# Splitting the inverse transform's turns and moving a weight load ahead in a mixer kernel

## The chip, the cores and the metric

The kernel runs on one core of a Trainium2 chip. The metric is device time in microseconds (us) of one execution, the median over several runs. The core has a matrix engine (TensorE, PE in the profile, its weight loads PEld), a vector engine (VectorE, DVE), an activation engine (ScalarE, ACT), a general engine (GpSimd, POOL), and a queue engine (SyncE, SP) that here issues nearly all DMAs. Every engine works through its own instructions in the order in which they were written. Results of TensorE go to PSUM, a small memory from which ACT and DVE copy them out ("evacuate" them) to SBUF.

## The reference

All inputs are fp32: a sequence of 2048 positions with 640 channels. Two blocks follow each other, each with a normalisation whose scale, shift and output factor come from a small product (`mod`, six rows of 640).

```
mod = silu(c) @ w_mod                  # sa, ca, ga, sb, cb, gb
h = layernorm(x) * (1 + ca) + sa
kv = shortconv(k, 4 taps) * v
y  = longconv(kv, ssm_k) + kv * ssm_D  # causal, 2048 taps, per channel, by FFT
x  = x + ga * (h * y)
h = layernorm(x) * (1 + cb) + sb
u = gelu(w1^T @ layernorm(h) + b1)     # along the positions: 2048 -> 1728
x = x + gb * (w2^T @ u + b2)           # 1728 -> 2048
```

## The kernel before

**Step one** makes the long convolution in 5 chunks of 128 channels (`for c in range(NC)`, c = 0 to 4; the last one has `cn is None`). Each chunk is a transform factored into 64 by 32 points. `step1` (products at L230) makes the first factor for the data (side 0) and for the filter (side 1), four turns each, and ACT copies each turn to the tile `z` (L235). `f2` (L249) makes the second factor in eight turns g = 0 to 7; ACT copies the filter's half (`kt`, L253), DVE multiplies (`mul`, tile `p`), and POOL or DVE adds up the complex product into the tile `y`. `i2` (products L279, copies L287) and `i1` (products L298) go back. `i2` is called twice per chunk, for r = 0 and 1: 128 products into two PSUM tiles of 128x1024 (`pp`), then four copies of 128x512 to `T2`, which lies in the tile `z`. The products of one `i2` go through s = 0 to 7, and s lies in blocks of 64 columns in each 512-column half of a tile. `i1` is called for both halves of the positions, 128 products into one PSUM tile each. Then `gate` (DVE) multiplies that tile with the normalised input `A1` (tile `aux`), and `add_x` adds the product to x. `a1_ops` makes `A1`: 16 ACT operations (L305), and on DVE the scale and shift (`po`, with the tile `g`). `fill` is a list of DVE operations that `dv(n)` takes n of at places written into the loop: the short convolution of a later chunk, and, from chunk 3 on, the statistics of the second normalisation (`x1s`, L524).

PSUM tiles come from a ring of three slots (`ring`); a fourth slot, `tap`, holds the sums of `mod_part` (L362), the product for `mod`. `i2` takes two slots, every other step one. Between the two calls of `i2` in chunks 1 to 3 stands one turn of `step1`. ACT also has, in these chunks, the copy `perm` (L176) of the next filter, which is written after the second turn of `step1` and before `i2(0)`.

**The last chunk** also loads the weights of step two. The first four blocks of 128 columns of `w1` are loaded as four row sets, r = 0 to 3, of 1 MB each (`load_rows` L416, set 0 in parts L544), and every set is split for each block f into a rounded part on ACT (L422) and a rest on DVE (`split_rows`, tiles `wb`). Set 0 goes to the tile `x`, set 1 to `aux`, set 2 to `z`, set 3 to `p` when that tile is no longer used.

**Step two** begins with the second block's normalisation: 16 row tiles j, each made by a chain of small operations (`stats`, `root_in`, `root`, `norm1`, `times`, `mean`, `plus`, `square`, `half`, `rest`; L716 to L764). Their order is written out by hand as a list of short names with arguments. `products` (Q, L445) multiplies two row tiles at a time with the four blocks of weights. Before the first Q stands a row of products whose result is not used (L804, 24 of them). After that come the other blocks of `w1`, the GELU, and the second product by seven multiplications in place of eight (L1086).

The order in all queues is that of the program (`manual_schedule`). Waits are put in by the framework, from what each instruction reads and writes.

## Time and profile before

| | |
|---|---|
| median of 3 runs | 682.18 us (678.96 to 683.72) |
| the profiled execution's own time | 679.36 us |
| its span, first to last instruction | 677.6 us |
| mean granted TensorE clock | 0.99 |
| PE busy | 629.8 us, 93% |
| DVE busy | 513.0 us, 76% |
| ACT busy | 316.0 us, 47% |
| POOL busy | 143.4 us, 21% |

All stamps are microseconds from the start of the span. A line of the chain of waits gives the start, the length, and the engine, tile and line that held the end of the program; "issue" is time in which the engine waited for nothing that the profile shows. A line of the timeline gives start, length, engine, line, operation, output and inputs with their shapes, the count, and in brackets the idle time of that engine before it and what ended this. A line of the windows gives, for a stretch of time, the busy time of PE, PEld, DVE, ACT and POOL (each with its count), the granted TensorE clock (1.00 is full), the share of the DMA engines and the GB/s that they moved.

Step one's chunks lie at about 23 to 100 (0), to 146 (1), to 196 (2), to 246 (3) and to 296 us (4); step two's Q runs from 306.05 us, and its second product from 506.61 us.

### The profile page before, as it was taken

The numbers are of one execution on the slowest core, as the hardware profiler recorded it, in microseconds if no ns is written. First come the engines' busy times: TensorE is split into PE (matmuls) and PEld (weight loads), VectorE is DVE, ScalarE is ACT, GpSimd is POOL, SyncE is SP. The second block draws the span as 40 slices with busy tenths as digits, with TensorE's granted clock in tenths as the row PEclk, the third lists the DMA queues.
The fourth block names the chain that finished last, engine by engine and source line by source line (L and its number), as shares of the span: only waits on it lengthen the run. The fifth ranks groups of instructions, "written<-read, shape, count | busy, mean of one in ns | idle before, by whom it ended". The sixth has DMA issues, their size and how long they took to land.

```text
span 677.6 us, 20710 instructions
## 1 busy us (share of the span) xinstructions
PE 629.8 (93%) x9057; PEld 611.8 (90%) x9057; DVE 513.0 (76%) x862; ACT 316.0 (47%) x483; POOL 143.4 (21%) x116
## 2 busy tenths in 40 slices
PE   0699888999999999889999999999999999999997
PEld 0699678999989989668999999999999999999997
DVE  7677689979978757879993312854679888888886
ACT  0574674745645546557875223433334333333331
POOL 5298039526327228200000000000000000000000
PEclk9999989999999999979999999999999999999999
DMA  9977987655432522634005540686499554355601
GB/s 188 217 219 237 369 147 152 156 95 136 85 69 86 165 63 69 180 86 102 2 1 108 116 88 1 166 221 172 143 345 304 176 178 121 114 160 167 182 34 40
DMA packets 173552, 95.91 MB, mean 142 GB/s; under 512 B 89715, under 2 KB 163222, under 8 KB 173462
## 3 DMA queue, kind: packets, MB, share of 16 engines
q1 hardware_dynamic: 168914, 93.28, 52.9%
q10 hardware_dynamic: 4548, 1.31, 1.1%
q8 instruction: 71, 1.16, 0.7%
q14 instruction: 19, 0.16, 0.1%
HBM read 77.53 MB, written 17.04 MB: 140 GB/s over the span
## 4 chain that ended last, share of the span: by engine, by line
PE 69%; DVE 17%; POOL 3%; issue 3%; DMA 3%; SPq 3%; ACT 2%; ACTq 0%; DVEq 0%; POOLq 0%
PE pst L1086 25%; PE pst L445 17%; PE pst L230 9%; PE pst L249 6%; PE pst L279 5%; PE pst L951 3%; DVE tap L60 3%; PE pst L298 2%; POOL y L60 2%; DVE p L60 2%; DVE kt L60 2%; SPq L166 1%; DVE x L60 1%; DMA in<-in_A_k_dram 1%; POOL t L60 1%
## 5 line engine op out<-in xcount | busy, mean ns | idle before, releaser
L249 PEld LDWEIGHTS pst<-z,w 128*64 128x64 f32 x2560 | 94.8, 141 | 5.8 <-ACT z L235 3.3
L249 PE MATMUL pst<-z,w 128*64 128x64 f32 x2560 | 96.1, 240 | 4.1 <-ACT z L235 2.1
L60 POOL TENSOR_TENSOR y<-p 128x256 f32<-128x256 f32 x68 | 89.4, 1366 | 25.6 <-DVE p L60 25.3
L230 PE MATMUL pst<-v,x 128*64 128x128 f32 x640 | 46.0, 303 | 25.4 <-DVE x L60 23.3
L230 PEld LDWEIGHTS pst<-v,x 128*64 128x64 f32 x640 | 43.9, 220 | 26.2 <-POOL t L470 23.2
L235 ACT ACTIVATE z<-pst 128x1024 f32<-128x1024 f32 (+2 forms) x45 | 46.5, 1046 | 41.8 <-PE pst L230 24.1
L60 DVE TENSOR_TENSOR p<-pst,kt 128x512 f32<-128x512 f32 x80 | 52.0, 692 | 15.2 <-ACT kt L253 8.7
L253 ACT ACTIVATE kt<-pst 128x512 f32<-128x512 f32 x40 | 25.3, 633 | 44.7 <-PE pst L249 25.3
L279 PEld LDWEIGHTS pst<-v,y 32*128 32x128 f32 x1280 | 38.7, 190 | 5.8 <-issue 3.9
L279 PE MATMUL pst<-v,y 32*128 32x64 f32 x1280 | 40.4, 275 | 3.2 <-issue 2.3
L230 PE MATMUL pst<-v,p 128*64 128x128 f32 x640 | 36.7, 274 | 2.4 <-ACT p L176 1.8
L230 PEld LDWEIGHTS pst<-v,p 128*64 128x64 f32 x640 | 35.0, 137 | 2.9 <-ACT p L176 1.9
L1086 PE MATMUL pst<-r_z,m_w 128*128 128x320 f32 x198 | 37.2, 309 | 0.0
L60 DVE TENSOR_TENSOR tap<-tap,kt 128x512 f32<-128x512 f32 x51 | 35.6, 697 | 1.3
L60 DVE TENSOR_TENSOR kt<-in,tap 128x512 f32<-128x512 f32 x51 | 35.1, 688 | 1.5
L1086 PEld LDWEIGHTS pst<-r_z,m_w 128*128 128x128 f32 x198 | 31.1, 188 | 0.1
L287 ACT ACTIVATE z<-pst 128x512 f32<-128x512 f32 x38 | 21.4, 664 | 19.6 <-PE pst L279 19.5
L1023 ACT ACTIVATE m_w<-m_v 128x896 fp32r<-128x896 f32 x19 | 17.9, 948 | 23.2 <-DVE m_v L60 13.1
L298 PEld LDWEIGHTS pst<-z,v 64*64 64x64 f32 x1280 | 23.0, 148 | 5.3 <-issue 2.5
L298 PE MATMUL pst<-z,v 64*64 64x64 f32 x1280 | 24.8, 233 | 1.9 <-issue 1.1
L855 ACT ACTIVATE pst<-pst,sm 128x640 f32<-128x640 f32 x14 | 10.7, 766 | 32.5 <-PE pst L445 32.5
L60 DVE TENSOR_TENSOR m_w<-m_v,m_w 128x896 fp32r<-128x896 f32 x19 | 20.6, 1087 | 6.5 <-ACT m_w L1023 6.5
(302 smaller groups left out, 1435.5 us busy)
## 6 DMA issues: line engine op xcount, KB each, us to landing
x<-in_B_w_dram SPq DMA_DIRECT2D x18, 512.0 KB
m_v<-in_B_w_dram SPq DMA_DIRECT2D x20, 384.0 KB
aux<-in_A_ssm_k_dram SPq DMA_DIRECT2D x10, 512.0 KB
out_dram<-m_w SPq DMA_DIRECT2D x32, 160.0 KB
in<-in_A_k_dram SPq DMA_DIRECT2D x36, 128.0 KB
in<-in_A_v_dram SPq DMA_DIRECT2D x36, 128.0 KB
ts<-m_p SPq DMA_DIRECT2D x10, 320.0 KB
m_w<-xs SPq DMA_DIRECT2D x20, 160.0 KB
```

Source lines behind the costliest of these rows:

```text
L60: TT = lambda eng, o, a, b, op: eng.tensor_tensor(o, a, b, op=op)
L230: pe.matmul(ps[64 * ri:64 * ri + 64, o:o + 128], lhs, F1[:, 128 * ri:128 * ri + 128], start=True, stop=True)
L235: act.activation(Z[:, side, t, :, k0:k1].rearrange("p a k e -> p e a k"), ps.rearrange("p (e a k) -> p e a k", a=8, e=2)[:, :, :, k0:k1], ...
L249: pe.matmul(ps[64 * h:64 * h + 64, o:o + 64], W2[k1 // 32][:, 2 * (k1 % 32) + ri], rhs, start=True, stop=True)
L253: act.activation(kt.rearrange("p (m i) -> p m i", i=32), pv[:, :, 1], AF.Copy)
L279: pe.matmul(pp[qd // 2][:, o:o + 64], Y[p, ri, i:i + 2].rearrange("p i k -> p (i k)"), V2[p, 64 * ri:64 * ri + 64], start=ri == 0, stop=ri ...
L287: act.activation(o, i, AF.Copy)
L298: pe.matmul(ps[64 * b:64 * b + 64, 512 * e + 64 * jj:512 * e + 64 * jj + 64], V1[p, ri, n2], T2[p, :, 32 * ri + n2], start=ri == 0, stop=r ...
L445: pe.matmul(ps[0:m, h, 0:320], w_.bitcast(F32R), r_[:, 320 * h:320 * h + 320].bitcast(F32R), start=first and i == 0, stop=last and i == 2)
L951: pe.matmul(ps[n][:, h, 0:320], sets[n][:, j].bitcast(F32R), r[:, 320 * h:320 * h + 320].bitcast(F32R), start=j == 0 and r is hh, stop=j = ...
L1023: act.activation(W[n][0].bitcast(F32R), A[p, w_], AF.Copy)
L1086: pe.matmul(bank[n], w[:, i].bitcast(F32R), r.bitcast(F32R), start=m == 0 and k == 0, stop=m == 6 and k == 2)
```

## The change

Five edits, all in step one and the entry of step two:

- `i2` in all chunks: the products go first through the even s (e = 0), then through the odd ones (e = 1), and after each half stand two copies of 128x512, one from each PSUM tile. Before, four copies stood at the end.
- Row sets 2 and 3 are copied in DRAM during chunk 3 to a new array `wc`, ordered so that one row of it holds all that a partition gets; set 2 in eight DMAs of 128 KB, set 3 in two of 512 KB. Set 2 is then loaded at turn 4 of the last chunk into the half of `w0` that later holds block 0's rests, and split in place (`split_third`); set 3 into `p` after the loop. The load of set 3 at the entry of step two goes. The `mod` load that was in `p` goes to `z`.
- In the last chunk's loop, ACT's `a1_ops` come three per turn, and `po` is taken from the loop's turns 4 to 7 (DVE) and no longer stands after the loop. 25 of the statistics move from the loop's first turns to the end of chunk 3.
- `i1(0)` of the last chunk comes in three parts (2, 3 and 3 of its 8 steps), with `mod_part` 3 and 4, `mod_sum` and `mod_row` placed between them. The gate and the add for the last three rows of this half, and the store of the half (`spill`), move into step two's list ("gr"); the add goes from DVE to POOL.
- In step two's list, the splits for block 2 ("v") and for row set 3 ("wh", "wl") stand at other places, three of the four "wh" on ACT are done earlier, and the unused products before Q are 40 in place of 24.

```
     def i2(r, eng=None):
         pp = [psum(), psum()]
...
+        for e in range(2):
+            for a in range(4):
+                for ri in range(2):
+                    for qd in range(4):
+                        p, s = slice(32 * qd, 32 * qd + 32), 2 * a + e
+                        o, i = 512 * (qd % 2) + 64 * s, 2 * (8 * r + s)
+                        pe.matmul(pp[qd // 2][:, o:o + 64], Y[p, ri, i:i + 2].rearrange("p i k -> p (i k)"),
+                                  V2[p, 64 * ri:64 * ri + 64], start=ri == 0, stop=ri == 1)
+            for n in range(2):
+                o = T2.rearrange("p (q a) m e -> p e q a m", a=8)[:, e, 2 * n:2 * n + 2, 4 * r:4 * r + 4]
+                i = pp[n].rearrange("p (q a e m) -> p e q a m", q=2, a=4, e=2)[:, e]
+                if eng is not None and n:
+                    eng.tensor_scalar(o, i, 1.0, None, op0=ALU.mult)
+                else:
+                    act.activation(o, i, AF.Copy)
...
+    THIRD = {0: 2, 1: 0, 2: 3, 3: 1}
+
+    def copy_rows(r, b, f=0, n=4):
+        o, step_ = (2048, 512) if r == 3 else (512 * THIRD[f], 128)
+        sync.dma_start(dram(wc, 64 * b * 4096 + o, [[4096, 64], [step_, 4], [1, 128 * n]]),
+                       dram(w1, (16 * b + 4 * r) * F + 128 * f, [[32 * F, 64], [F, 4], [1, 128 * n]]))
+
+    def split_third(f, hi=True, lo=True):
+        n = THIRD[f]
+        t, (h_, l_) = blk[0][1][:, 4 * n:4 * n + 4], (t_[:, 8:12] for t_ in blk[f])
+        if hi:
+            act.activation(h_.bitcast(F32R), t, AF.Copy)
+        if lo:
+            TT(dve, l_.bitcast(F32R), t, h_, ALU.subtract)
...
+            if cn == NC - 1:
+                copy_rows(2, g % 2, g // 2, 1)
+                if g in (3, 6):
+                    copy_rows(3, g // 6)
...
-                dv(4 if g else len(fill) - 16)
-                if g == 5:
+                dv(len(fill))
+                if g == 4:
                     t = mem("w0", 4096, "wb0")
                     blk[0] = j16(t[:, 0:2048]), j16(t[:, 2048:4096])
-                if g in (5, 7):
-                    split_rows(1, T_aux[:, 0:2048], (0,), g == 5, g == 7)
+                    sync.dma_start(t[:, 2048:4096], wc[:, 0:2048])
+                if g >= 4:
+                    po.pop(0)()
+                if g == 6:
+                    split_rows(1, T_aux[:, 0:2048], (0,), True, False)
+                if g == 7:
+                    split_third(0)
+                    split_rows(0, X, (0,), True, False)
...
-            load_rows(2, T_z[:, 1920:3968])
-            mod_load(3, 4, P[:, 0:1920])
+            mod_load(3, 4, T_z[:, 1920:3840])
+            sync.dma_start(P, wc[:, 2048:4096])
...
-            split_rows(0, X, (0, 1, 3))
-            split_rows(1, T_aux[:, 0:2048], (1, 3))
-            run(po)
+            for f in (1, 3):
+                split_third(f)
+                split_rows(0, X, (f,))
+                split_rows(1, T_aux[:, 0:2048], (f,))
+            split_rows(0, X, (0,), False, True)
+            split_rows(1, T_aux[:, 0:2048], (0,), False, True)
         if c:
...
             i2(0)
             if cn is None:
-                split_rows(2, T_z[:, 1920:3968], (0, 1, 3), True, False)
-                split_rows(2, T_z[:, 1920:3968], (0, 1), False, True)
+                split_rows(3, P, (1, 3))
+                split_rows(3, P, (0,), True, False)
+                i2(1, dve)
                 mod_part(tap, 3, pl[3])
-                i2(1, dve)
...
-            dv(3)
+            dv(3 if cn < NC - 1 else 28)
...
-    mod_part(tap, 4, pl[4])
-    ps0 = i1(0)
+    ps0 = i1(0, jjs=range(2))
     s0, s1, s2 = ((uid[0] + i) % 3 for i in range(3))
-    mod_sum(tap, T_t[:, 0:640])
     gate(NC - 1, ps0, 0, dve, 0, 2)
     run(lambda j=j: stats(j) for j in (0, 1))
+    split_rows(0, X, (2,), True, False)
+    split_rows(1, T_aux[:, 0:2048], (2,), True, False)
+    split_third(2, True, False)
+    mod_part(tap, 4, pl[4])
+    i1(0, ps=ps0, jjs=range(2, 5))
+    mod_sum(tap, T_t[:, 0:640])
     root_in(0)
-    gate(NC - 1, ps0, 0, None, 2, 8)
+    gate(NC - 1, ps0, 0, None, 2, 5)
     root(0)
-    add_x(NC - 1, 0, dve, 2, 8)
-    spill(NC - 1, (0,))
-    load_rows(3, P)
+    add_x(NC - 1, 0, dve, 2, 5)
...
+    i1(0, ps=ps0, jjs=range(5, 8))
     ps = i1(1, s1)
...
-    for i in range(24):
+    for i in range(40):
...
+    def rest_of_half():
+        gate(NC - 1, ps0, 0, None, 5, 8)
+        add_x(NC - 1, 0, pool, 5, 8)
+        spill(NC - 1, (0,))
...
-            t 0 1 m 0 w2 0 p 0 1 s 0 1 st 2 3 q 1 gb 0 R 1 n 2 3 h 0 1
+            t 0 1 m 0 v 0 p 0 1 s 0 1 st 2 3 q 1 gr 0 gb 0 R 1 n 2 3 h 0 1
...
```

More of the change, by code (lines that the diff above doesn't have):

```diff
@@ L68, in mixer_kernel @@
     ts = drp.tile([5 * 128, 2560], F32, name="ts")
+    wc = drp.tile([128, 4096], F32, name="wc")
     ring = [0, 1, 2]
@@ L273, in i2, with i1 @@
         pp = [psum(), psum()]
[L274 to L292 removed]
+        for e in range(2):
[13 more added lines that the diff above has]
+                    act.activation(o, i, AF.Copy)
+    def i1(half, slot=None, ps=None, jjs=range(8)):
+        if ps is None:
+            ps = psum(slot)
+        for jj in jjs:
             for ri in range(2):
@@ L537, in mixer_kernel @@
             if c:
-                for f_ in ac[2 * g:2 * g + 2]:
-                    f_()
+                n_ = 2 if cn is not None else 3
+                for f_ in ac[n_ * g:n_ * g + n_]:
+                    f_()
+            if cn == NC - 1:
+                copy_rows(2, g % 2, g // 2, 1)
+                if g in (3, 6):
+                    copy_rows(3, g // 6)
             if cn is None and g < 4:
```

37 lines of the change are left out of this document (10 added, 27 removed).

## The prediction

> **What bounds the kernel now.** I read the page first, then the chain of waits in order of time, and then the timelines of single engines where the change touches them.
>
> ```profile
> span 677.6 us, 20710 instructions
> PE 629.8 (93%) x9057; PEld 611.8 (90%) x9057; DVE 513.0 (76%) x862; ACT 316.0 (47%) x483; POOL 143.4 (21%) x116
> ```
>
> The kernel itself took 679.36 us, its span 677.6 us. PE is busy for 93% of the span, so a change must free time in which PE waits, or in which it can't yet begin with what only PE limits. The chain of waits (start, length, engine, tile, line, count) shows both kinds. First chunk 3, which is as chunks 1 and 2, and then the end of the last chunk:
>
> ```profile
> 224.24 2.28 PE pst L230 x32
> 226.52 3.73 PE pst L279 x128
> 230.25 2.24 PE pst L230 x32
> 232.49 3.93 PE pst L279 x128
> 236.42 2.23 PE pst L230 x32
> 238.65 2.02 PE pst L298 x118
> 240.67 0.89 issue
> ...
> 275.04 3.58 PE pst L279 x120
> 278.62 1.21 PE tap L362 x12
> 279.83 2.06 PE pst L279 x63
> 281.88 2.26 issue
> 284.14 2.90 PE pst L279 x63
> 287.04 2.29 PE tap L362 x12
> 289.32 3.25 PE pst L298 x128
> ...
> 292.59 0.44 DVE aux L60
> ```
>
> In chunk 3 the chain is PE alone: a turn of `step1` (L230), `i2(0)` (L279), a turn, `i2(1)`, a turn, `i1` (L298), without a gap up to a stop of 0.89 us that the profile gives to no engine. Whatever PE loses here, the kernel loses. At the end of the last chunk PE also holds the chain, up to the first gate on DVE at 292.59 us. From there small DVE and ACT steps lead to the first product of step two. In the next fence the first two lines are from PE's timeline, the last from the windows (span, then busy time of PE, with its count).
>
> ```profile
> 298.77 5.28 PE L804 MATMUL pst<-wb,wb 128*128 128x320 f32 x24 [1.68 <-ACT kt L387]
> 306.05 7.33 PE L445 MATMUL pst<-r_z,wb 128*128 128x320 f32 x48 [1.99 <-ACT r_z L761]
> ...
> 352.00:420.00 68.00, 68.00 (x465) 67.99 (x464) 20.70 (x34) 23.71 (x37) 0.00 (x0) 1.00 0.41 78
> ```
>
> Step two's products begin at 306.05 us; from 352 to 420 us PE is busy for 68.00 of 68.00 us. So the gain that the change can make is the time by which the first product comes earlier, as long as DVE follows.
>
> **Part 1, the waits inside `i2`.** The change adds two copies between the two halves of each `i2`. They read the tiles into which the second half then writes, other columns of the same 512-column halves. The trace of before has no place where PE writes columns of a PSUM tile while another engine reads other columns of it. So the cost has two ends. If PE need not wait, it is nothing; it is not less, since behind both calls in chunks 1 to 3 PE goes on with a turn of `step1` at once and a shorter tail of copies releases nothing. If PE waits, it costs the two copies and whatever is queued ahead of them on ACT. The nearest rows for a PE write to a tile that ACT is emptying are these, ACT and then PE:
>
> ```profile
> 68.25 1.08 ACT L235 ACTIVATE z<-pst 128x1024 f32<-128x1024 f32 x1 [0.70 <-PE pst L230]
> ```
> ```profile
> 69.37 3.79 PE L279 MATMUL pst<-v,y 32*128 32x64 f32 x124 [0.62 <-ACT z L235]
> ```
>
> The copy ends at 69.33 us and PE goes on at 69.37 us. PE waits for the whole reading operation, and starts 0.04 us behind it. I take this end, the full wait. The Trainium skill ("PSUM — Partial Sum Buffer", section "PSUM bank collisions raise a hardware error") speaks against the change: engines must be kept apart by bank and quadrant, not by address, because an access to other columns of the same bank collides all the same. By that rule the wait stands in all ten calls and the sum is the one below, +8.4 us. By the rows alone it may also be nothing, -5.8 us in all, and that is the first rival.
>
> ACT in chunk 3:
>
> ```profile
> 227.55 2.09 ACT L176 ACTIVATE p<-aux 128x2048 f32<-128x2048 f32 x1
> 230.28 2.30 ACT L287 ACTIVATE z<-pst 128x512 f32<-128x512 f32 x4 [0.64 <-PE pst L279]
> ...
> 236.28 2.26 ACT L287 ACTIVATE z<-pst 128x512 f32<-128x512 f32 x4 [2.65 <-PE pst L279]
> ```
>
> The first half of `i2(0)` is half of 3.73 us: it ends at 226.52 + 1.87 = 228.39 us. ACT is then in `perm` until 227.55 + 2.09 = 229.64 us, which stands ahead of the copies. Two of the four copies take half of 2.30, 1.15 us, to 230.79 us; the second half of the products ends at 232.66 us, against 230.25 us before: +2.41 us. For `i2(1)` ACT is free (it waited 2.65 us for PE), so two copies of 2.26 / 2 = 1.13 us are added. One chunk loses 3.54 us. `perm` is of one size in all chunks:
>
> ```profile
> L176 ACT ACTIVATE p<-aux 128x2048 f32<-128x2048 f32 x5 | 10.5, 2096 | 1.8 <-POOL aux L60 1.8
> ```
>
> Chunks 1 to 3 have the same order, so they lose 3 x 3.54 = 10.6 us. Everything behind (gate, short convolution, the next chunk's `f2`) starts from `i1`, so it moves along.
>
> In chunk 0, PE and then ACT:
>
> ```profile
> 78.28 3.80 PE L279 MATMUL pst<-v,y 32*128 32x64 f32 x128
> ```
> ```profile
> 80.36 1.65 ACT L305 ACTIVATE aux<-xa,sm 128x128 f32<-128x128 f32 x4 [1.60 <-DVE sm L351]
> 82.11 2.17 ACT L287 ACTIVATE z<-pst 128x512 f32<-128x512 f32 x4
> ```
>
> The first half of `i2(1)` ends at 78.28 + 1.90 = 80.18 us; ACT is in four operations of `a1_ops` until 82.01 us, the two copies (half of 2.17) end at 83.10 us, the second half at 85.0 us instead of 82.08 us: 2.9 us for `mod_part` 4 and what hangs on it, `A1` and the gate. The short convolution behind these waits a little for data anyway:
>
> ```profile
> 99.91 0.70 DVE L60 TENSOR_TENSOR tap<-in,tap 128x512 f32<-128x512 f32 x1 [0.78 <-DMA in<-in_A_k_dram]
> ```
>
> That takes 0.78 us off, and the DVE work between leaves some slack. `i2(0)` of this chunk loses about 1.1 us ahead of products of `mod` that wait for their own loads. Bounds 0 and 2.9 us; I take 1.3 us, a little under the middle, because of these two covers.
>
> **Part 2, the last chunk up to the gate.** DVE gets `po` in turns 4 to 7, that is four operations for which it took 4.87 us after the loop. In the next fence are DVE's rows and then POOL's.
>
> ```profile
> 269.44 1.33 DVE L60 TENSOR_TENSOR p<-pst,kt 128x512 f32<-128x512 f32 x2 [1.01 <-POOL y L60]
> ...
> 271.76 1.29 DVE L60 TENSOR_TENSOR p<-pst,kt 128x512 f32<-128x512 f32 x2 [0.40 <-ACT kt L253]
> 272.97 2.52 DVE L60 TENSOR_TENSOR y<-p 128x128 f32<-128x128 f32 x4
> ...
> 278.42 4.87 DVE L60 TENSOR_TENSOR aux<-aux,g 128x1024 f32<-128x1024 f32 x4
> ```
> ```profile
> 256.06 18.59 POOL L60 TENSOR_TENSOR y<-p 128x256 f32<-128x256 f32 x14 [6.17 <-DVE p L60]
> ```
>
> A turn of `f2` lasts about 2.4 us (14 additions of POOL, seven turns, in 18.59 us make 2.66 us), the multiplication takes 1.3 us of DVE and one `po` 1.22 us: DVE is just full, but POOL sets the pace, and DVE waited 1.01 us for it at 269.44 us. At turn 7 DVE then has the multiplication (to 270.7), `po` (to 272.0) and a split that waits for ACT (to 272.9 or so) before the last multiplication, which began at 271.76 us. About 1.2 us late, its first two additions (two of the four in 2.52 us) end near 275.5 us; POOL ends at 274.65 us. So `i2(0)` starts at 275.6 instead of 275.04 us.
>
> From there by the rows of the first fence: first half 1.87, copies 1.15, second half 1.87 to 280.5 us. `i2(1)` needs a slot that a further copy empties (0.6): 281.1, first half to 283.0. Its copies on ACT stand behind three splits of row set 3 (1.67 us, below), 281.7 to 283.4 us, so they end at 284.0, the second half at 285.9. Then `mod_part` 3 at 1.21 us, and a quarter of an `i1`, at most a quarter of 3.25 us but at the full clock nearer 0.5: the gate starts at 287.7 us instead of 292.59 us, 4.9 us earlier. What went: `mod_part` 4 ahead of the gate (2.29 us), three quarters of `i1`, the stop of 2.26 us, and the time at half clock that followed it (below, last row). DVE's ten rests and `po` before took until the gate with pauses; now eight of them run beside `i2(0)`.
>
> ACT must not wait for set 3. Before, ACT waited 0.52 us for set 2, in `z`:
>
> ```profile
> 281.38 1.67 ACT L422 ACTIVATE wb<-z 128x512 fp32r<-128x512 f32 x3 [0.52 <-DMA z<-in_B_w_dram]
> ```
> ```profile
> 271.44 1.29 SPq L416 DMA_DIRECT2D z<-in_B_w_dram  x2
> ```
>
> Set 2 was issued from 271.44 us and in use at 281.38 us, ten microseconds for 1 MB beside two loads for `mod`. In the windows (last three figures: clock, DMA share, GB/s), the whole rows of `mod` went at 412 GB/s, the set in pieces of 2 KB at 227 GB/s, with the DMA engines full in both:
>
> ```profile
> 274.00:275.00 1.00, 0.71 (x14) 0.31 (x8) 1.00 (x2) 1.00 (x2) 0.66 (x1) 1.00 1.04 412
> ...
> 277.00:278.00 1.00, 1.00 (x45) 1.00 (x43) 1.00 (x3) 0.00 (x0) 0.00 (x0) 1.00 1.07 227
> ...
> 287.00:288.00 1.00, 1.00 (x9) 0.35 (x9) 0.89 (x2) 0.95 (x2) 0.00 (x0) 0.50 0.00 0
> ```
>
> Now `p` is free at about 276.8 us, and a partition's 8 KB lie in one piece: by 412 GB/s 1 MB takes 2.6 us, and with 2 us that I allow for its start and landing (an estimate, no row here shows it) the set is there near 281.5 us, just in time. Were it like the pieces, it would land after 283 us; each microsecond then counts, since `i2(1)`'s copies stand behind it on ACT and DVE, and PE and the gate behind those.
>
> The copies in DRAM cost SP ten issues at 0.64 us (two in 1.29 us), 6.4 us in chunk 3, ahead of `mod` loads that are first read after the last chunk's loop; a whole `f2` covers them. The early load of set 2 lies between the loads of set 0 and turn 7 and replaces that of 271.44 us. The statistics go where DVE waits for `i1`. All these at nothing; if a load were late, ACT would wait as above.
>
> **Part 3, the entry of step two.** The gate's last three rows are now in front of the square roots that the first product needs: by 0.44 us for two rows about 0.6 us. Their add goes to POOL, idle there, and the store behind it has one later job on SP, the load into `x`. The copy of `mod_row` 4 on ACT now stands closer ahead of `norm1`, for which I put 0.3 us. Together +0.9 us. Three splits fewer on ACT relieve no bound. Forty unused products at 0.15 to 0.22 us (48 in 7.33, 24 in 5.28 us) are 6.1 to 8.8 us from about 295 us on, so they end between 301 and 304 us; Q comes at 306.05 - 4.9 + 0.9 = 302.0 us, which may be hit. A stop like that of 2.26 us can come again. I allow 0.5 us: part 2 and 3 give -3.5 us, bounds -6 and +1.
>
> **The sum.** 10.6 + 1.3 - 3.5 = +8.4 us on 679.36 us: 687.8 us for a profiled execution. The three runs before have their median 2.8 us above it, at 682.18 us, so I forecast 690.6 us. From its bounds this case alone spans 685 to 696 us.
>
> **The rivals.** *No wait in `i2`:* PE writes the odd blocks while the even ones are read. For it speaks that the columns differ, against it the row at 69.37 us. The rule of the Trainium skill above (PSUM — Partial Sum Buffer) speaks against it too. Part 1 is then nothing, and the gate starts at 275.6 + 3.73 + 0.6 + 3.73 + 1.21 + 0.5 = 285.4 us, 7.2 us earlier; with +0.9 and the 0.5 us it is -5.8 us, 676.4 us. It decides as soon as the stops between halves are under 0.6 us each (5.8 us over ten). Chance 0.17.
>
> *The waits are there, but half covered:* the stops of "issue" as at 240.67 us vanish in PE's new pauses (up to 2.7 us in three chunks), chunk 0 hides its part, and the last chunk keeps 4.5 us: 10.6 - 2.7 - 4.5 = +3.4 us, 685.6 us. For it speaks that something fetched late is fetched anyway; against it that the stop comes after the pauses. Chance 0.20.
>
> *Set 3 comes late:* with the ten microseconds of set 2 it lands at 287 us, the copies end at 289.6, the gate starts at 293.2 us: +0.6 + 0.9 instead of -3.5 us, +13.4 us, 695.6 us. The change then doesn't do what it says. Against it stands the 412 GB/s. Chance 0.10.
>
> **The numbers.** The forecast has 0.53. About 1%, 6.8 us, is what a measurement of this kernel can tell from no change: 675.4 and 689.0 us. Half of the first rival lies below, 0.09 faster. Its other half 0.08, most of the second 0.17 and a third of the forecast 0.18 make 0.43 within 1%. The rest, 0.48, is slower. The range of 680 to 697 us holds the forecast, the second and third rival, and leaves out the first.
>
> **What would show it.** Right: PE waits at L279 for ACT's L287 in every call, 1.2 us for most and 2.4 us behind `perm`; chunks 1 to 3 each some 3.5 us longer; the last chunk's gate and Q some 4 us nearer to the end of its `f2`. Wrong: L279 without such waits and a shorter span; or ACT at the splits of `p` waiting for a DMA; or PE full with unused products when Q's inputs are ready.

## The result and the profile after

The changed kernel took 722.0 us in the median (718.4 to 724.1, four runs); the kernel before, on the same chip, 681.3 us (679.0 to 683.7). The ratio is 1.058, with an interval of 1.055 to 1.062. The sign of the forecast was right; its size was not: +40.7 us were measured where 8.4 us were forecast. The profiled execution took 724.14 us, 2.1 us above the median, and its span is 722.3 us.

The head of the page of the changed kernel, with the granted clock in 40 slices:

```profile
span 722.3 us, 20735 instructions
PE 664.0 (92%) x9073; PEld 639.6 (89%) x9073; DVE 519.0 (72%) x863; ACT 316.0 (44%) x483; POOL 147.6 (20%) x117
PEclk9999789979969969957999999999999999999999
```

PE has 16 instructions more than before (the unused products), but is busy for 34.2 us more. So most of the loss is not waiting: the same products take longer. The last line says where: the clock falls in the slices up to the entry of step two, at each `i2`, and stands at 9 behind it.

The stages, from the starts of the first `f2` of each chunk and of the first product Q in PE's timelines (before: 102.26, 152.84, 202.03, 251.92, 306.05; after: 109.89, 167.38, 225.50, 283.40, 347.24):

| stage | before, us | after, us | difference | forecast |
|---|---|---|---|---|
| up to `f2` of chunk 1 (chunk 0) | 102.3 | 109.9 | +7.6 | +1.3 |
| chunk 1 | 50.6 | 57.5 | +6.9 | +3.5 |
| chunk 2 | 49.2 | 58.1 | +8.9 | +3.5 |
| chunk 3 | 49.9 | 57.9 | +8.0 | +3.5 |
| last chunk, `f2` to Q | 54.1 | 63.8 | +9.7 | parts 2 and 3: |
| Q to the end | 371.5 | 375.1 | +3.5 | -3.5 in all |
| span | 677.6 | 722.3 | +44.7 | +8.4 |

**Chunks 1 to 3.** The view of waits of the changed kernel (engine, tile, line, what it waited for: us in total, times, the longest):

```profile
PE pst L281 <- ACT z L289: 9.8, 11, 1.7
PE pst L281 <- DVE y L60: 6.2, 1, 6.2
PE pst L464 <- DVE wb L60: 2.5, 1, 2.5
```

The first line is the forecast wait, PE ahead of the second half of `i2` (L281) for ACT's copies (L289). It is there: 9.8 us in eleven places, the ten second halves and one start of `i2(1)`. This view counts only the time up to the first product behind the wait. PE's timeline in chunk 3 shows what else there is:

```profile
250.08 2.01 PE L281 MATMUL pst<-v,y 32*128 32x64 f32 x64
253.80 4.17 PE L281 MATMUL pst<-v,y 32*128 32x64 f32 x64 [1.71 <-ACT z L289]
257.91 3.52 PE L231 MATMUL pst<-v,x 128*64 128x128 f32 x32
261.35 2.01 PE L281 MATMUL pst<-v,y 32*128 32x64 f32 x64
264.07 4.17 PE L281 MATMUL pst<-v,y 32*128 32x64 f32 x64 [0.70 <-ACT z L289]
268.17 3.51 PE L231 MATMUL pst<-v,x 128*64 128x128 f32 x32
271.62 2.10 PE L301 MATMUL pst<-z,v 64*64 64x64 f32 x128
```

Each first half takes 2.01 us, each second half, with the same 64 products, 4.17 us. The turn of `step1` behind it takes 3.5 us, where the timeline of the kernel before has 2.31 and 2.30 us (2.24 and 2.23 in its chain). The windows of the same stretch (the last three figures: granted clock, DMA share, GB/s) give the reason:

```profile
252.00:254.00 2.00, 0.29 (x8) 0.20 (x4) 2.00 (x1) 2.00 (x3) 0.00 (x0) 1.00 0.04 8
254.00:256.00 2.00, 1.94 (x36) 1.80 (x38) 1.97 (x2) 0.25 (x1) 0.00 (x0) 0.57 0.60 129
256.00:258.00 2.00, 2.00 (x38) 1.88 (x34) 2.00 (x10) 0.37 (x1) 0.00 (x0) 0.50 1.09 255
...
262.00:264.00 2.00, 1.37 (x52) 1.23 (x44) 0.00 (x0) 1.16 (x3) 0.00 (x0) 1.00 0.03 8
264.00:266.00 2.00, 1.87 (x32) 1.73 (x32) 0.00 (x0) 0.52 (x2) 0.00 (x0) 0.63 0.00 0
266.00:268.00 2.00, 2.00 (x40) 2.00 (x36) 0.00 (x0) 0.10 (x1) 0.00 (x0) 0.50 0.00 0
```

Behind each pause the clock falls to half. Windows that are cut where it changes show for how long:

```profile
254.28:261.11 6.83, 6.81 (x90) 6.69 (x92) 6.83 (x26) 1.18 (x2) 0.00 (x0) 0.50 0.70 154
261.11:264.52 3.41, 2.69 (x74) 2.26 (x70) 0.74 (x4) 2.21 (x3) 0.00 (x0) 1.00 0.02 5
264.52:271.35 6.83, 6.78 (x90) 6.67 (x92) 0.00 (x0) 1.15 (x2) 0.00 (x0) 0.50 0.01 2
```

The waits themselves are about as long as forecast. ACT in the same place, and PE's weight loads (PEld), which stand ahead of the products:

```profile
251.18 2.06 ACT L177 ACTIVATE p<-aux 128x2048 f32<-128x2048 f32 x1
253.12 1.13 ACT L289 ACTIVATE z<-pst 128x512 f32<-128x512 f32 x2
263.40 1.12 ACT L289 ACTIVATE z<-pst 128x512 f32<-128x512 f32 x2 [0.84 <-PE pst L281]
```
```profile
253.80 0.30 PEld L281 LDWEIGHTS pst<-v,y 32*128 32x128 f32 x4 [1.85 <-ACT z L289]
254.30 3.49 PEld L281 LDWEIGHTS pst<-v,y 32*128 32x128 f32 x60 [0.20 <-ACT z L289]
264.57 3.49 PEld L281 LDWEIGHTS pst<-v,y 32*128 32x128 f32 x60 [0.20 <-ACT z L289]
```

The two copies take 1.13 us from 253.12 us. PE goes on at 253.80 us, when the first of them ends, but with four products only; then it waits for the second copy, out of the other tile, which ends at 254.25 us, and goes on for good at 254.30 us. In `i2(1)` the copies end at 264.52 us and PE goes on for good at 264.57 us. From the ends of the first halves, 252.09 and 263.36 us, that is 2.2 + 1.2 us; less 0.13 us for each group of four products, PE loses 3.2 us by waiting.

The sum for chunk 3: waits 3.2 us; slower second halves, 60 products in 3.67 us (254.30 to 257.97, 264.57 to 268.24) where 2.01 x 60 / 64 = 1.88 us would do, twice 1.79 = 3.6 us; slower turns 3.52 + 3.51 - 2.31 - 2.30 = 2.4 us. That is 9.2 us, of which 6.0 us are the half clock. Less the stop of 0.89 us within `i1` that chunk 3 of this execution hasn't, it is 8.3 us, beside the 8.0 in the table.

**The last chunk.** DVE's timeline in turns 4 to 7 of the loop:

```profile
295.09 1.68 DVE L60 TENSOR_TENSOR aux<-aux,g 128x1024 f32<-128x1024 f32 x1
296.68 1.28 DVE L60 TENSOR_TENSOR p<-pst,kt 128x512 f32<-128x512 f32 x2
297.89 2.61 DVE L60 TENSOR_TENSOR aux<-aux,g 128x1024 f32<-128x1024 f32 x1
300.43 1.30 DVE L60 TENSOR_TENSOR p<-pst,kt 128x512 f32<-128x512 f32 x2
301.64 4.49 DVE L60 TENSOR_TENSOR aux<-aux,g 128x1024 f32<-128x1024 f32 x1
306.05 1.27 DVE L60 TENSOR_TENSOR p<-pst,kt 128x512 f32<-128x512 f32 x2
307.25 1.71 DVE L60 TENSOR_TENSOR aux<-aux,g 128x1024 f32<-128x1024 f32 x1
308.88 1.53 DVE L60 TENSOR_TENSOR wb<-wb 128x512 fp32r<-128x512 f32 x1
310.33 1.27 DVE L60 TENSOR_TENSOR p<-pst,kt 128x512 f32<-128x512 f32 x2
```

`po` (aux<-aux,g) took 1.22 us each behind the loop; here it takes 1.68, 2.61, 4.49 and 1.71 us. A split of 0.68 us takes 1.53 us. The multiplications between them, one input of which is in PSUM, keep their 1.3 us. The last one begins at 310.33 us, 7.9 us behind the end of `f2` (283.40 + 19.03 = 302.4 us); before, it was 0.8 us. PE waits for it, and its clock falls:

```profile
312.03 3.69 PE L281 MATMUL pst<-v,y 32*128 32x64 f32 x64 [6.24 <-DVE y L60]
```
```profile
310.00:312.00 2.00, 0.00 (x0) 0.00 (x0) 2.00 (x5) 0.00 (x0) 0.00 (x0) 0.50 0.00 0
...
330.00:332.00 2.00, 2.00 (x33) 0.88 (x31) 0.00 (x0) 0.92 (x2) 0.00 (x0) 0.50 0.00 0
332.00:334.00 2.00, 2.00 (x45) 0.92 (x42) 1.39 (x5) 0.10 (x1) 0.00 (x0) 0.80 0.00 0
```

Both `i2` and the beginning of `i1` run at half clock. The gate starts at 332.51 us, 30.1 us behind the end of `f2` (before: 292.59 - 270.97 = 21.6 us). From gate to Q it is 14.7 us (before: 13.5). In step two PE waits once more, 2.46 us, for a rest of block 2 on DVE (the last line of the waits above).

### The profile page after: what moved, and what is told of

Read it like the earlier page. It is cut to its first block, busy times and chain, and to the rows that moved or that the text cites. A ratio compares the mean times of both kernels' runs of the same rounds, so it can differ in the third digit from the quotient of the medians.

```text
span 722.3 us, 20735 instructions
## 1 busy us (share of the span) xinstructions
PE 664.0 (92%) x9073; PEld 639.6 (89%) x9073; DVE 519.0 (72%) x863; ACT 316.0 (44%) x483; POOL 147.6 (20%) x117
## 4 chain that ended last, share of the span: by engine, by line
PE 67%; DVE 18%; ACT 4%; SPq 3%; DMA 3%; issue 3%; POOL 2%; ACTq 0%; DVEq 0%; POOLq 0%
PE pst L1128 23%; PE pst L464 18%; PE pst L231 8%; PE pst L281 6%; PE pst L250 4%; PE pst L993 3%; DVE tap L60 3%; DVE p L60 3%; DVE kt L60 2%; POOL y L60 2%; PE pst L301 2%; DVE aux L60 2%; PE tap L365 1%; ACT z L289 1%; SPq L167 1%
## 5 line engine op out<-in xcount | busy, mean ns | idle before, releaser
L60 POOL TENSOR_TENSOR y<-p 128x256 f32<-128x256 f32 x68 | 91.2, 1396 | 31.8 <-DVE p L60 31.6
L231 PE MATMUL pst<-v,x 128*64 128x128 f32 x640 | 53.6, 338 | 25.7 <-DVE x L60 23.2
L281 PE MATMUL pst<-v,y 32*128 32x64 f32 x1280 | 61.3, 342 | 17.1 <-ACT z L289 9.8
L281 PEld LDWEIGHTS pst<-v,y 32*128 32x128 f32 x1280 | 56.8, 250 | 22.1 <-ACT z L289 13.0
L231 PEld LDWEIGHTS pst<-v,x 128*64 128x64 f32 x640 | 51.1, 222 | 26.8 <-POOL t L489 23.2
L289 ACT ACTIVATE z<-pst 128x512 f32<-128x512 f32 x38 | 21.8, 628 | 44.1 <-PE pst L281 44.1
L60 POOL TENSOR_TENSOR xa<-xa,aux 128x1024 f32<-128x1024 f32 (+1 forms) x4 | 8.2, 2056 | 108.5 <-DVE aux L60 108.5
L60 DVE TENSOR_TENSOR aux<-aux,g 128x1024 f32<-128x1024 f32 (+1 forms) x14 | 30.0, 2148 | 0.2
L60 DVE TENSOR_TENSOR x<-tap,in 128x512 f32<-128x512 f32 x17 | 11.8, 691 | 23.2 <-PE pst L231 22.8
```

The costliest lines, as they stand in the source:

```text
L60: TT = lambda eng, o, a, b, op: eng.tensor_tensor(o, a, b, op=op)
L231: pe.matmul(ps[64 * ri:64 * ri + 64, o:o + 128], lhs, F1[:, 128 * ri:128 * ri + 128], start=True, stop=True)
L281: pe.matmul(pp[qd // 2][:, o:o + 64], Y[p, ri, i:i + 2].rearrange("p i k -> p (i k)"), V2[p, 64 * ri:64 * ri + 64], start=ri == 0, stop=ri ...
L289: act.activation(o, i, AF.Copy)
```

## The experiments

The theory from this profile: the loss has two independent sources, the split of `i2`, which costs mostly clock, and `po` in the loop, which DVE and POOL fight over. Its rivals: the waits in `i2` alone; the new order of the products; a DVE that simply has too much to do in turns 4 to 7; and a loss that lies in step two.

**The split of `i2` alone.** The kernel before, with the `i2` of the change and nothing else of it:

```
-        for s in range(8):
-            for ri in range(2):
...
-        for qd in range(4):
+        for e in range(2):
+            for a in range(4):
+                for ri in range(2):
...
+            for n in range(2):
```

> The kernel before with one edit: i2's products go through the even and then the odd blocks, with two copies after each half. Theory W (the wait alone costs, as the forecast had it): chunks 1 to 3 lose 3.5 us each, chunk 0 1 to 3 us, the last chunk 1 to 3 us: 13 to 16 us slower than before, about 695 us, and the granted clock stays at 1.00 behind the waits. Theory C (PE's clock halves behind each wait and stays so for the second half and the next turn of step1): chunks 1 to 3 lose about 9 us each, chunk 0 about 6, the last chunk 3 to 6: 35 to 40 us slower, about 718 us, clock 0.50 in most of 3.5 us windows behind a wait. Rival T (the two edits at the last chunk are the main cost): under 10 us slower.

It took 714.58 us, beside 681.76 us for the kernel before: ratio 1.0475 (1.0434 to 1.0516), +32.8 us. That is four fifths of the loss, far above what waits alone would give and just under what waits with the clock were to give.

**The other edits alone.** The changed kernel, with the `i2` of the kernel before:

```
-        for e in range(2):
-            for a in range(4):
...
+        for s in range(8):
+            for ri in range(2):
...
+        for qd in range(4):
```

> The changed kernel with i2 as it was before; all other edits stay. The forecast's theory for them: 4 to 6 us faster than before, first product of step two 4 to 6 us nearer to the end of the last f2. Theory P (DVE's scale and shift of A1 in turns 4 to 7 and POOL's additions hold each other up): those DVE operations take 1.7 to 4.5 us instead of 1.22 us also here, i2(0) of the last chunk starts 8 to 10 us behind the end of f2 instead of 4, PE's clock halves in that gap, and the time is 5 to 12 us slower than before.

It took 690.1 us, ratio 1.013 (1.008 to 1.018), +8.3 us. 32.8 + 8.3 = 41.1, and both together had +40.7 us: the two add up. Of the forecast, -5.8 us belong to the other edits (its case without waits), and 8.4 + 5.8 = +14.2 us to the split. `po` took 1.36 to 2.55 us here, and `i2(0)` of the last chunk started 7.4 us behind the end of `f2`: less than the 8 to 10 us expected, more than the 4.1 us of the kernel before (275.04 - 270.97).

**The order of the products without the waits.**

```
         for e in range(2):
             for a in range(4):
...
+        for e in range(2):
             for n in range(2):
```

That is `i2_split` with all four copies behind both halves.

> The kernel before, with the products of i2 in the new order (even blocks, then odd) but all four copies at the end, so that nothing waits between the halves. Theories W and C: no difference from before, within 2 us. If the order of the products or the new form of the copies itself cost something (128x512 from every second block of 64 columns), it is slower by what i2_split is, or by a part of it, and L289-like copies are longer than 0.58 us each.

It took 681.53 us, ratio 0.9997 (0.9969 to 1.0025). Neither the order of the products nor the form of the copies costs anything. It is the place of the copies.

**Something to do in the pause.** `i2_split` with five products of 128x256 between the halves, written to the next slot of the ring, whose result is not used:

```
+        dum = psp.tile([128, 1024], F32, name=f"dum_{uid[0]}", tag=f"pst{ring[(uid[0] + 1) % len(ring)]}", bufs=1)
         for e in range(2):
+            for _ in range(5 * e):
+                pe.matmul(dum[:, 0:256], SM[:, 0:128], SM[:, 0:256], start=True, stop=True)
```

> The kernel i2_split with five unused products of 128x256 on PE between the halves of each i2, into a PSUM tile that nobody reads; about 1.3 us, so PE works while ACT copies. The waits for the copies stay. Theory C: the clock stays at 1.00 and only the waits cost, 13 to 18 us slower than before, so about 20 us faster than i2_split. Theory W: the clock was never the matter; like i2_split within 3 us, or slower by up to 4 us where five products take longer than the copies.

It took 700.02 us, ratio 1.026 (1.021 to 1.031): 14.6 us faster than `i2_split`, by doing more. Its PE timeline in chunk 3:

```profile
238.60 2.01 PE L283 MATMUL pst<-v,y 32*128 32x64 f32 x64
240.55 2.42 PE L277 MATMUL dum<-v 128*128 128x256 f32 x10
242.90 2.01 PE L283 MATMUL pst<-v,y 32*128 32x64 f32 x64
244.85 2.28 PE L230 MATMUL pst<-v,x 128*64 128x128 f32 x32
```

The second half takes 2.01 us and the turn 2.28 us; the clock is 1.00 in every window from 238 to 254 us. The unused products last 2.42 us, more than the 2.2 and 1.2 us for which the copies hold PE up, where 1.3 us were expected. So what is left, 18.3 us against the 13 to 18 expected, is mostly their own length (ten calls of up to 2.4 us); the half clock had cost more than they do.

**A short pause.** `i2_split` with the copies between the halves cut to one column of four. Three quarters of the even blocks' copies are left out, so the time is one without this work.

```
+                if not e:
+                    o, i = o[:, :, :, 0:1], i[:, :, :, 0:1]
```

> i2_split (32.8 us slower than before) with the copies between the two halves cut to one column of four, so the output is not the reference's: three quarters of the even blocks' copies are left out. PE still waits for them between the halves, but behind an idle ACT only some 0.3 to 0.5 us instead of 0.7; in `i2(0)` of chunks 1 to 3 it still waits for `perm` on ACT, some 1.3 us. Length theory (the granted clock falls only for pauses of 0.7 us and more): it stays full in `i2(1)`, 12 to 18 us slower than before, 694 to 700 us. Any-pause theory (the clock falls at any wait inside these small products): half clock behind each of the waits as in i2_split, 22 to 30 us slower than before, 704 to 712 us.

It took 695.47 us, ratio 1.0195 (1.014 to 1.025), +13.6 us, in the range of the theory by length. PE in chunk 3:

```profile
240.69 2.17 PE L280 MATMUL pst<-v,y 32*128 32x64 f32 x64 [1.26 <-ACT z L290]
242.78 3.50 PE L230 MATMUL pst<-v,x 128*64 128x128 f32 x32
246.21 2.01 PE L280 MATMUL pst<-v,y 32*128 32x64 f32 x64
248.49 2.07 PE L280 MATMUL pst<-v,y 32*128 32x64 f32 x64 [0.27 <-ACT z L290]
250.49 2.31 PE L230 MATMUL pst<-v,x 128*64 128x128 f32 x32
```

Behind 1.26 us (`perm` stands ahead of the copies) the clock falls, later than in `i2_split`; behind 0.27 us it doesn't.

**`po` back behind the loop.** The other edits alone, with this one of them undone:

```
-                if g >= 4:
-                    po.pop(0)()
...
             split_rows(1, T_aux[:, 0:2048], (0,), False, True)
+            run(po)
```

> rest_alone with one part undone: the four `po` run after the loop of the last chunk, in one piece behind the splits, as in the kernel before. rest_alone was 8.3 us slower than before. Port theory (two inputs in SBUF on DVE while POOL adds block one another: `po` took up to 2.55 us in rest_alone, and POOL's 14 additions 22.05 us instead of 18.59 us): POOL's additions back to 18 to 19 us, `i2(0)` starts 4 to 5 us behind the end of `f2` instead of 7.5, PE's clock stays full there, and the time falls by 5 to 9 us against rest_alone, to 681 to 685 us. Theory of the full DVE (turns 4 to 7 simply hold more DVE work than a turn lasts): the same here; the next run tells the two apart. If neither `po` nor the clock is the cause (the loss lies in step two): within 2 us of rest_alone, 688 to 692 us.

It took 683.36 us, ratio 1.0021 (0.9994 to 1.0047), 6.7 us less in the median than with `po` in the loop, in the range. POOL's fourteen additions took 18.44 us (22.05 with `po` in the loop). This alone doesn't say whether DVE was full or blocked.

**`po` in the loop, with one input from PSUM.** ACT copies the 2 x 128 columns of `g` that `po` needs to columns 512 to 767 of `tap`, which are free until the first product of `mod`; DVE has the same operations at the same places (`g0` and `g1` are the two halves of `GP`, in the last chunk alone):

```
+    GP = tap[:, 512:768].rearrange("p (n m) -> p n m", n=2)
...
-    TT(dve, a, a, gh(G1), ALU.mult), TT(dve, a, a, gh(G0), ALU.add)
+    TT(dve, a, a, g1, ALU.mult), TT(dve, a, a, g0, ALU.add)
...
+            if cn is None and g == 0:
+                act.activation(GP, T_g.rearrange("p (n m) -> p n m", n=2)[:, :, c * DC:(c + 1) * DC], AF.Copy)
```

> rest_alone with `po` left in turns 4 to 7, but its rows of G0 and G1 (128 columns each) are copied by ACT into free columns of the PSUM tile `tap` in turn 0, so each `po` has one input in SBUF and one in PSUM. DVE has the same operations at the same places. Port theory: each `po` takes 1.2 to 1.4 us, POOL's 14 additions 18 to 19.5 us, `i2(0)` starts 4 to 5.5 us behind the end of `f2` at full clock, the time is 6 to 10 us below rest_alone, 680 to 684 us. Theory of the full DVE: `po` still delays the multiplications, POOL needs 21 us or more, `i2(0)` 7 us or more behind `f2`, and the time stays within 2 us of rest_alone, 688 to 692 us.

It took 684.96 us, ratio 1.0052 (1.0033 to 1.0071), 5.1 us less than with both inputs in SBUF. DVE's timeline:

```profile
267.59 1.22 DVE L60 TENSOR_TENSOR aux<-aux,tap 128x1024 f32<-128x1024 f32 x1
268.75 1.30 DVE L60 TENSOR_TENSOR p<-pst,kt 128x512 f32<-128x512 f32 x2
269.96 1.23 DVE L60 TENSOR_TENSOR aux<-aux,tap 128x1024 f32<-128x1024 f32 x1
271.10 1.28 DVE L60 TENSOR_TENSOR p<-pst,kt 128x512 f32<-128x512 f32 x2
```

Same work, same turns: 1.22 us each, and POOL's additions 18.46 us. A full DVE is ruled out as the cause; two inputs in SBUF while POOL adds is it. The Trainium skill ("SBUF — State Buffer", section "Who interferes with whom") has this rule: a DVE instruction with two SBUF inputs contends with a GpSimd instruction that reads SBUF, and with at most one, outside the two-port modes, it does not. The trace agrees, 1.22 against 4.49 us. From the start of the last `f2` to Q it is 53.5 us, against 59.8 in `rest_alone`: 6.4 us less, in the range. The whole gain lies a little under it. In the profiled execution this kernel was 1.6 us behind `rest_alone` already when that `f2` started (255.91 against 254.32 us), ahead of any `po`. The first product of `mod` also waited 0.97 us for the last `po`, which reads the same PSUM tile.

**The rest of block 2 earlier in step two.**

```
-  ... s 8 9 t 10 r 7 Q 3 ...  st 15 t 12 v 2 r 8 9 Q 4
+  ... s 8 9 v 2 t 10 r 7 Q 3 ...  st 15 t 12 r 8 9 Q 4
```

> rest_alone with one word of step two's list moved: the rests of block 2 for row set 2 (`v 2`) come two lines of the list earlier, ahead of `t 10`, instead of just ahead of `Q 4`, where PE waited 2.46 us for them. If it is only their place: that wait goes and 1.5 to 2.5 us with it, 687.6 to 688.6 us. If DVE is full over the whole stretch, the wait moves to another operation of DVE, and the time stays within 0.7 us of rest_alone.

The time, 689.23 us (685.3 to 690.8) beside 690.1 us, settles nothing: 0.9 us lies inside their spread. The profile does. The wait at `Q 4` is gone, and from Q to the end it is 688.9 - 317.34 = 371.6 us, as in the kernel before (371.5), against 688.7 - 314.14 = 374.6 us. In the profiled execution `po` took up to 4.53 us, 2.55 us in the other one, and `f2` to Q was 2.0 us longer for it.

**Without what was found.** From here on the question was whether the edits other than the split of `i2` are worth something when freed of these costs. `rest_late` and `rest_psum` each got two moves: `v 2` as above, and `mod_part` 3 back between the two `i2`, so that PE works while ACT empties the slot that `i2(1)` needs (a pause of 1.0 us, then half clock: `i2(1)` took 7.09 us). In `best_psum` the rest that stood ahead of the loop's last multiplication also went behind the loop.

```
             i2(0)
             if cn is None:
+                mod_part(tap, 3, pl[3])
                 split_rows(3, P, (1, 3))
...
                 i2(1, dve)
-                mod_part(tap, 3, pl[3])
```

> rest_late (683.4 us; before 681.8) with two more moves: `v 2` two lines earlier in step two's list, as in rest_v, and `mod_part` 3 back between `i2(0)` and `i2(1)`, as in the kernel before. In rest_late PE waits 1.01 us there for ACT's copies, and `i2(1)` then takes 7.09 us instead of about 3.8 at half clock. Clock theory: PE works through these 1.2 us, the pause shrinks to under 0.4 us and the clock stays full: 1.0 + 3.3 us for it and 2.4 us for `v 2`, 676 to 678.5 us, 0.5 to 0.9% faster than before. If the clock falls in the last chunk in any case (the short pause left over, or a stop of issue as in the kernel before): only `v 2` and some of the pause, 680 to 681.5 us.

> rest_psum (685.0 us) with the same two moves, and the one rest that stood ahead of the last multiplication of the loop put behind it. Clock theory: as best_late, and `i2(0)` some 1 us nearer to the end of `f2`; `i2(1)` waits for no queue on DVE, so the gate comes 1 to 2 us earlier than in best_late: 675 to 678.5 us. If the clock falls in any case: 680 to 682 us. If the stops of issue decide, which differ from kernel to kernel (rest_psum stood 2.4 us later than rest_late already at the start of the last chunk): 1 to 2 us above best_late.

They took 682.28 us, ratio 0.9993 (0.9965 to 1.002), and 680.48 us, ratio 0.9972 (0.9945 to 0.9999). `i2(1)` now took 3.91 and about 4.2 us, as expected, but the pause moved on: ahead of `i1` PE waited 3.98 us in the first (DVE has the 4.87 us of `po` ahead of its copies) and 1.52 us in the second, and the clock fell there. So both lie where a clock that falls in any case would put them, or a little above (680 to 681.5 and 680 to 682 us), and not where a full clock would.

**Two more moves on it.** `mod_part` 4 ahead of `i1`, and `po` one turn earlier:

```
+    mod_part(tap, 4, pl[4])
     ps0 = i1(0, jjs=range(2))
...
-                if g >= 4:
+                if 3 <= g < 7:
                     po.pop(0)()
```

> best_psum (680.5 us, 2.2 us below before in its own call) with two moves more: `mod_part` 4 runs ahead of the first `i1` instead of behind its first two indices, so PE has work while ACT and DVE copy the second half of `i2(1)` (in best_psum a pause of 1.52 us, and then half clock until 291 us); and `po` in turns 3 to 6 instead of 4 to 7, so the first product of `mod` doesn't wait 1.03 us for the last `po`, which reads the same PSUM tile. Clock theory: the pause falls under 0.5 us and the clock stays full, 1.0 to 1.8 us for it, and 0.3 to 0.8 us for `po`: 677.5 to 679.5 us where before is at 682.2, ratio 0.993 to 0.997. If the pause costs nothing because DVE sets the gate: `po` alone, 0.996 to 0.998, as best_psum.

It took 678.41 us, ratio 0.9954 (0.9927 to 0.998), as expected in its size, though its interval overlaps that of `best_psum`; not in its reason: the pause ahead of `i1` was still 1.42 us and the clock still fell. What came last there was ACT:

```profile
285.96 1.67 ACT L447 ACTIVATE wb<-p 128x512 fp32r<-128x512 f32 x3 [2.14 <-DMA p<-wc]
287.54 1.11 ACT L288 ACTIVATE z<-pst 128x512 f32<-128x512 f32 x2
```

ACT waits for row set 3, issued at 278.52 us, until 285.96 us, and the copies of `i2(1)` are queued behind. That is 7.4 us from issue to use, where the forecast had 4.6.

**The splits of set 3 later.** Behind the second part of the gate:

```
-                split_rows(3, P, (1, 3))
-                split_rows(3, P, (0,), True, False)
...
     add_x(NC - 1, 0, dve, 2, 5)
+    split_rows(3, P, (1, 3))
+    split_rows(3, P, (0,), True, False)
```

> best_both (678.4 us, before in its call 682.0, ratio 0.9954) with the splits of row set 3 (three copies on ACT, two rests on DVE) moved from between the two `i2` to behind the add of the second gate part. In best_both ACT waits 2.14 us for this set's load until 285.96 us, and the copies of the second half of `i2(1)`, queued behind its splits, end about 1 us after PE; PE then pauses 1.42 us ahead of `i1` and falls to half clock until 296 us. Theory of the late set: the copies follow `i2(1)` at once, the pause is under 0.5 us, the clock stays full, the first product of step two comes 1 to 2.5 us earlier against the end of `f2`: 676 to 677.5 us, ratio 0.990 to 0.994. If ACT's queue behind (the copies of block 2, the copy of `mod`'s sum) is the bound: the splits only move along the same chain, ratio 0.994 to 0.998.

It took 677.44 us, ratio 0.9934 (0.9905 to 0.9964): the lowest ratio of this study, 4.5 us below the kernel before by it; the changed kernel was 40.7 us above. The interval overlaps that of `best_both`, so the gain of this last move is not shown by the times. ACT's wait is gone, and the pause ahead of `i1` was 0.31 us. But the clock did not stay full in the profiled execution (681.49 us, 4 us above its median):

```profile
290.66 0.69 PE L300 MATMUL pst<-z,v 64*64 64x64 f32 x32 [0.31 <-DVE z L286]
291.89 0.93 PE L300 MATMUL pst<-z,v 64*64 64x64 f32 x48 [0.54 <-DVE aux L60]
```
```profile
294.00:296.00 2.00, 2.00 (x62) 1.58 (x64) 1.90 (x7) 2.00 (x5) 0.00 (x0) 0.50 0.00 0
```

Two short pauses of 0.31 and 0.54 us, 0.69 us apart, were the only ones ahead of this fall. Behind them come products of a single row (`mod_row`, 1x320); whether they have a share in it, no run separates. That part of the expectation fell.

## Why the prediction was wrong

**What bounds the kernel: right.** PE holds the chain in chunks 1 to 3, and what it loses there is lost: 9.2 us less the 0.89 us stop in chunk 3, where the chunk became 8.0 us longer.

**Part 1, the waits: right that they come and nearly right in how long they are, wrong in what they cost.** PE waits at each second half for the copies, as the row at 69.37 us had it, and the rule of the Trainium skill ("PSUM — Partial Sum Buffer", section "PSUM bank collisions raise a hardware error") speaks for the same; the rival without waits is out. The wait that the prediction summed, the two copies and what is queued ahead of them on ACT, 3.54 us a chunk, measured 3.2 us in chunk 3. The step that failed is the one from there to "One chunk loses 3.54 us": it put the second half at 1.87 us, its length at full clock, and the turn behind it at no change. Behind each wait the clock falls to half, and in chunk 3 that costs another 6.0 us for the slower halves and turns. `i2_busy` shows this by filling the pause, `i2_tiny` by shortening it. The prediction had the evidence in hand: it quoted a window at clock 0.50 behind the stop of 2.26 us and took that time off in part 2. It did not ask what the new pauses of part 1 would do. In chunk 0, for which it took 1.3 us between 0 and 2.9, the loss was 7.6 us: pauses of 0.54 and 0.70 us, and behind each of them products of `i2`, `mod` and `i1` at half clock. The upper bound failed for the same reason. (The span of 685 to 696 us that the prediction states is, from its own terms, 687 to 697 us; both are far from 722.)

**Part 2: the step that failed is "one `po` 1.22 us: DVE is just full, but POOL sets the pace".** The 1.22 us came from behind the loop, where POOL is idle. Beside POOL's additions the four took 10.5 us in place of 4.87. So `i2(0)` started 9.6 us behind the end of `f2`, where 4.6 us were forecast (270.97 to 275.6), and at half clock; the gate came 8.5 us later in place of 4.9 us earlier. `rest_psum` shows the cause: the same four operations at the same places take 1.22 us when one input lies in PSUM.

"ACT must not wait for set 3": in the changed kernel it didn't, since all else was later still, so the late set 3 did not come about there. With the costs of `po` taken away it did: ACT waited 1.36 us for it in `rest_late`, 1.00 in `rest_psum` and 2.14 in `best_both`, there 7.4 us from issue to use. The forecast's "just in time" was too tight by about that.

"`mod_part` 4 ahead of the gate" was counted as time that goes. What the kernel before had in it was cover: `mod_part` 3 and 4 ran in pauses of PE. Moved out of them, the pauses stay, 1.0 us ahead of `i2(1)` in `rest_late`, and with them the half clock.

**Part 3: nearly right at the entry, with a term left out behind it.** Gate to Q became 1.3 us longer, 0.9 was forecast. The rests of block 2, which before ran ahead of the gate, were put at nothing in step two; that was the 2.46 us wait at `Q 4`, most of the 3.5 us from Q to the end. `rest_v` shows that it was only their place: DVE had room for them two lines earlier.

**The rivals.** No wait, and waits half covered, fell with the eleven waits of the profile; a late set 3 was not what happened. None of them, nor the forecast, had the clock in it as a cost of the new waits, so no case came near +40 us.

**The sum in hindsight.** The split of `i2` costs +32.8 us where +14.2 was forecast (11.9 in chunks 0 to 3, the rest in the last chunk), and the other edits +8.3 where -5.8 was. With `po`, `v 2`, the two `mod_part` and the splits of set 3 put right, the other edits are worth -4.5 us (by the interval -2.5 to -6.5): a gain of the size that parts 2 and 3 looked for is there, but only behind these repairs.

## What to carry to other kernels

A wait put into a run of small products is priced with the clock that it may cost, not only with its length: look in the windows of the old profile for what the granted clock did behind pauses of that kind, and give PE something to do in the gap or leave the gap out. A duration is taken from a row with the same neighbours: an operation of DVE with both inputs in SBUF, moved beside a busy POOL, is not the same operation. And work that looks like a delay ahead of the critical step may be the cover of a pause; before it is moved out, say what fills its place.

## What the runs showed that was not expected

**The clock falls behind very short pauses.** In `i2` (32-row products of 64 columns) a pause of 0.70 us, with a shorter one behind the next four products, was followed by 6.8 us at half clock, in chunks 1 to 3; in chunk 0 one of 0.54 us was enough, with one of 0.63 us a little ahead of it. At 0.27 us (`i2_tiny`) it held. The length alone isn't the rule: in the kernel before, pauses of 0.89 us and 1.08 us between other products (ahead of 241.56 and 224.24 us) left the clock at 1.00, and in `set3_later` 0.31 and 0.54 us close together did not.

The clock also changes only in fixed steps. In each of the fourteen profiles, all of its changes lie on one grid of 3.41 us: the half-clock stretches of the changed kernel that end within the program last 3.41, 6.83, 10.24 or 23.89 us, and the full ones between 261.11 and 264.52 us or 271.35 and 308.90 us are whole multiples of 3.41 us too. So the half clock behind a pause lasts for whole steps, and where the pause lies on the grid decides which products are slow: the same `i2` in chunk 3 has a second half of 4.17 us and a turn of 3.52 us in the changed kernel, and 3.48 and 3.69 us in `i2_split`. PE's busy share of the step ahead isn't the rule either: from 261.11 to 264.52 us PE is busy for 2.69 of 3.41 us, and the clock falls; in the kernel before, from 240.68 to 244.09 us, it is busy for only 2.53 us, with products of 64 and 128 rows in place of 32, and the clock stays at 1.00.

The Trainium skill ("TensorE: Matmul & The Clock Gate", section "HAM oscillation — how this bites in real kernels") warns of idle gaps over about 3.4 us; the pauses here are well under that, and the measurement decides. Its section "What's actually happening" says that the activity window runs freely, so that the point of the change varies from run to run. That fits the grid, and also that the twelve executions of `set3_later` have mean granted clocks from 0.976 to 0.997 with one and the same program. But no run of this study changes the place on the grid or the kind of product alone; what exactly sets the fall stays open.

**PSUM columns borrowed in a shared tile still cost.** In `rest_psum` PE's first product of `mod` waited 0.97 us for the last `po`, which reads columns 512 to 767 of `tap`. That product writes columns 0 to 319, so the wait is of the same kind as in `i2`, put in where nobody had asked for it; but the products of `mod` right behind it write columns 512 to 831, and some of it was due in any case.
